# Zero products in one run, seven normalised tiles on ScalarE and seven centred tiles on VectorE, in a transformer block on one core

## The chip, the cores and the metric

One core of a Trainium2 chip. The metric is the device time in microseconds (us) of one execution; a profile's span, from the first to the last instruction, is somewhat shorter. The engines work side by side and meet at semaphores: TensorE (PE, matrix products; PEld is its loading of weights), VectorE (DVE), ScalarE (ACT), GpSimd (POOL), and SyncE (SP), which issues all transfers here.

## The reference

A pre-norm block: linear attention with a learned feature map (32 heads of 20), then a bilinear gated layer. Sequence 2048, width 640, inner width 1536, bf16.

```python
def _layernorm(x, axis=-1, eps=1e-5):
    m = jnp.mean(x, axis=axis, keepdims=True)
    v = jnp.var(x, axis=axis, keepdims=True)
    return (x - m) / jnp.sqrt(v + eps)

    # A: attention, with q, k, v = x @ wqkv, split in heads
    pk = jnp.einsum("bhsd,hdf->bhsf", k, w_phi)           # the same for q
    phi_k = jnp.concatenate([_softmax(pk), _softmax(-pk)], axis=-1)
    kv = jnp.einsum("bhsf,bhsd->bhfd", phi_k, v)
    z  = jnp.einsum("bhsf->bhf", phi_k)
    num = jnp.einsum("bhqf,bhfd->bhqd", phi_q, kv)
    den = jnp.einsum("bhqf,bhf->bhq", phi_q, z)[..., None] + 1e-6
    o = num / den                                         # heads joined, then @ wo

    # B: gated layer
    g = jnp.einsum("bsd,df->bsf", x, w_gate)
    u = jnp.einsum("bsd,df->bsf", x, w_up)
    return jnp.einsum("bsf,fd->bsd", g * u, w_down)

    h = x + _A_ref(_layernorm(x), A_wqkv, A_w_phi, A_wo)
    h2 = h + _B_ref(_layernorm(h), B_w_gate, B_w_up, B_w_down)
```

## The kernel before

The sequence is cut into 16 tiles of 128 rows. The program is a graph of named operations, each with an engine and the buffers that it reads and writes. A list scheduler in Python, which runs while the kernel is built, puts them into one fixed order for each engine, and derives the semaphore waits from it. What it goes by is a table with an entry for each operation: a key (a smaller key goes first among the operations that are ready) and, after a second colon, which of its allowed engines it takes (0, the default, is the one it is declared with, 1 the alternative). `xn3:13.372` is the normalisation of tile 3 with key 13.372 on its declared engine.

The names that matter here: `x` loads of rows, `wk`, `wv` loads of weights, `warm` products of zeros whose result nobody reads, `PH` and `PS` small products that lay the feature weights out, `WT` transposes of wk blocks on TensorE, `F1` folds of the feature weights into wk, `L1` statistics of the first layernorm, `xn` its normalised rows, `xt` their transpose (on TensorE for tiles 0 to 2, by a DMA from tile 3 on), `V`, `K`, `KV` the projections and the product of keys and values, `hc` the centred rows of the second layernorm, `hT` their transpose by DMA, `U` and `D` the gated layer.

TensorE's first operations, with cuts:

```python
NWARM = 8
def warm(e):
    for _ in range(1):
        ins = e.matmul(pb(wm_b)[:, 0:512], lhsT=T["zero"][:, 0:P], rhs=T["zero"][:, :], start=True, stop=True)
    return ins
for k in range(NWARM):
    G.op("pe", "warm%d" % k, warm, 0.43 if k < 7 else 0.22, LT, [z_b], [wm_b], -90)
# ...
G.op("pe", "PH", rows, 1.9, LT, [w32_b, id_b], [pq_b], -95)      # 40 products of 16 columns
# PHd: a copy of PH's result into phid
G.op("pe", "PS", spread, 0.6, LT, [es_b, pd_b], [pr_b], -95)     # 14 products
# PHe: a copy of PS's result into Phi; WT0..4, F1_0..4 follow
```

With the table of before, TensorE runs warm0 to warm3, PH, warm4 to warm6, PS, WT0, WT1, xt1, WT4, xt0, warm7, and then the folds F1 and the first V.

The first layernorm. VectorE makes mean and variance of each tile, ScalarE the reciprocal root as exp(-0.5 ln(v + eps)) for a group of up to four tiles, VectorE the normalised rows:

```python
G.op("dve", "L1s%d" % t, l1, ...)                   # two bn_stats over 320 columns each
G.op("dve", "L1a%d" % t, ...)                       # bn_aggr -> mv[t] = mean, variance
for tl in LNG:                                      # [0] [1] [2,3] [4..7] [8..11] [12..15]
    G.op("act", "L1l%d" % a, ...)                   # Ln
    G.op("act", "L1e%d" % a, ...)                   # Exp -> rs
def xn(e, t=t, xb=xb):
    return e.tensor_scalar(out=rev(xb), in0=T["x"][:, t, :].rearrange("p (c n) -> p c n", c=NC),
                           scalar1=T["mv"][:, t, 0:1], scalar2=T["rs"][:, t:t + 1], op0=ALU.subtract, op1=ALU.mult)
G.op("dve", "xn%d" % t, xn, 0.5, LD, [x_b[t], mv_b[t], rs_b[t]], [xb], 10 * t - 22)
```

The second layernorm. The rows are only centred here (mean minus row); the scale comes in at the end, when the gated layer's result is multiplied by 1/(v + eps), since the layer is of second degree in its input.

```python
G.op("act", "hc%d" % t, lambda e, t=t, hc=hc: e.activation(
    out=rev(hc), in_=T["x"][:, t, :].rearrange("p (c n) -> p c n", c=NC), func=AF.Identity, scale=-1.0, bias=T["mv2"][:, t, 0:1]),
    act_c(640, True), LA, [x_b[t], m2], [hc], kk)
```

`xn` and `hc` share four row buffers. All transfers, the transposes by DMA among them, are issued by SyncE in one fixed order, so an issue that waits for its data holds those behind it.

Of the kernel before, what the change touches and what calls it, by code (L numbers as in the profile page):

```python
# [6 lines left out]
FP32 = mybir.dt.float32  # L7
# [5 lines left out]
P = 128  # L13
# [29 lines left out]
NWARM = 8  # L43
# [5 lines left out]
x0:1.66 wk0:2.14 wk2:4.06 wk4:2.62 x1:1.18 wv0:3.58 wv2:4.54 wv4:5.98 x2:3.1 x4:5.02 x6:5.5 w32:0.7 x8:15.272 x10:22.162 x12:29.242 x14:21.682  # L49
wqt0:25.582 wqt1:26.802 wqt2:34.322 wqt3:35.542 wqt4:39.202 wqt5:40.422 wo0:55.782 wo2:58.182 wg0:55.302 wu0:56.742 wg1:54.822 wu1:57.222 wg2:53.382  # L50
wu2:57.702 wg3:54.342 wu3:58.662 wg4:53.862 wu4:56.262 id0:0.95 gl0:0.7 eps:1.25 id1:1.45 gla0:4.88 glb0:5.25 gla4:4.22 glb4:4.66 gla1:2.67 glb1:4.44
gla2:2.89 glb2:3.33 gla3:3.11 glb3:3.8 va1:1.85 glx:5.62 kv1:6.02 zero:0.7 warm0:1.08 warm1:1.51 warm2:1.94 warm3:2.37 warm4:4.7 warm5:5.13 warm6:5.56
warm7:8.153 es0:3.55 es1:4.02 PH:2.8 PHd:4.97 PS:5.99 PHe:6.86 WT0:6.59 WTe0:7.483 WT1:6.925 WTe1:8.213:1 WT2:10.4 WTe2:11.005:1 WT3:10.735
WTe3:11.657:1 WT4:7.539 WTe4:8.144:1 F1_0:8.423 Fe1_0:9.567:1 F1_1:9.227 Fe1_1:10.813 F1_2:12.157 Fe1_2:12.728:1 F1_3:13.002 Fe1_3:13.574 F1_4:8.809
Fe1_4:10.19:1 L1s0:4.686 L1a0:5.686 L1s1:3.823 L1a1:5.506 L1s2:9.867 L1a2:10.867 L1s3:9.047 L1a3:10.687 L1s4:11.732 L1a4:15.192 L1s5:12.552 L1a5:16.761
L1s6:15.302 L1a6:16.541 L1s7:14.372 L1a7:16.651 L1s8:26.422 L1a8:28.172 L1s9:20.982 L1a9:29.812 L1s10:25.602 L1a10:27.242 L1s11:27.352 L1a11:29.702
L1s12:38.952 L1a12:40.592 L1s13:39.772 L1a13:43.052 L1s14:40.702 L1a14:42.942 L1s15:30.382 L1a15:32.702 L1l0:6.016 L1e0:6.446 L1l1:5.796 L1e1:6.236
L1l2:11.437 L1e2:12.387 L1l4:17.051 L1e4:17.894 L1l8:30.102 L1e8:30.532 L1l12:43.63 L1e12:44.06 xn0:7.046 xt0:7.874 xte0:8.629:1 xn1:6.546 xt1:7.26
xte1:8.943 xn2:13.872 xt2:15.205 xte2:16.122:1 xn3:13.372 xt3:14.052 xn4:19.062 xt4:20.462 xn5:24.642 xt5:28.022 xn6:18.562 xt6:19.242 xn7:23.682
xt7:24.362 xn8:31.702 xt8:33.102 xn9:32.202 xt9:37.982 xn10:31.202 xt10:31.882 xn11:34.232 xt11:36.762 xn12:46.002 xt12:46.942 xn13:50.762 xt13:52.162  # L60
xn14:45.042 xt14:45.722 xn15:50.262 xt15:50.942 V0_0:9.777 V0_1:10.048 V0_2:11.342 V0_3:11.885 V0_4:13.847 Ve0:14.82 K0_0:15.484 K0_1:15.756
K0_2:16.028 K0_3:16.299 K0_4:16.571 Kx0_0:17.271 Kx0_1:18.104 Ks0:19.562 Kr0:21.802 Kn0:22.442 KV0:30.426 V1_0:11.07 V1_1:11.613 V1_2:12.458 V1_3:12.73
V1_4:13.304 Ve1:14.197 K1_0:13.575 K1_1:14.119 K1_2:14.39 K1_3:14.662 K1_4:14.934 Kx1_0:15.475 Kx1_1:16.309 Ks1:17.142 Kr1:25.142 Kn1:27.181 KV1:31.102
V2:16.843 Ve2:18.727 K2:18.201 Kx2_0:19.83 Kx2_1:20.663 Ks2:22.262 Kr2:24.182 Kn2:24.822 KV2:34.495 V3:19.56 Ve3:21.286 K3:20.918 Kx3_0:22.546
Kx3_1:23.38 Ks3:28.282 Kr3:29.922 Kn3:30.562 KV3:39.246 V4:26.351 Ve4:28.078 K4:24.993 Kx4_0:26.621 Kx4_1:27.455 Ks4:34.732 Kr4:37.572 Kn4:38.212
KV4:42.639 V5:33.137 Ve5:34.863 K5:31.778 Kx5_0:33.407 Kx5_1:34.24 Ks5:36.152 Kr5:38.032 Kn5:40.571 KV5:43.315 V6:23.635 Ve6:25.46 K6:22.276
Kx6_0:24.003 Kx6_1:24.836 Ks6:32.812 Kr6:38.492 Kn6:42.93 KV6:45.651 V7:29.068 Ve7:30.696 K7:27.71 Kx7_0:31.372 Kx7_1:32.206 Ks7:41.522 Kr7:43.162
Kn7:45.289 KV7:50.402 V8:36.529 Ve8:38.158 K8:39.922 Kx8_0:41.55 Kx8_1:42.384 Ks8:46.502 Kr8:49.342 Kn8:50.007 KV8:55.153 V9:41.28 Ve9:43.007 K9:44.292
Kx9_0:45.921 Kx9_1:46.754 Ks9:47.922 Kr9:49.802 Kn9:52.366 KV9:57.49 V10:35.171 Ve10:36.799 K10:37.888 Kx10_0:39.516 Kx10_1:40.349 Ks10:43.622
Kr10:45.542 Kn10:47.648 KV10:58.166 V11:46.327 Ve11:47.955 K11:47.685 Kx11_0:49.313 Kx11_1:50.147 Ks11:51.262 Kr11:54.102 Kn11:54.742 KV11:61.86  # L70
V12:51.078 Ve12:52.706 K12:52.437 Kx12_0:54.065 Kx12_1:54.898 Ks12:56.175 Kr12:58.511 Kn12:59.46 KV12:62.536 V13:58.842 Ve13:60.47 K13:55.829
Kx13_0:57.458 Kx13_1:58.291 Ks13:59.124 Kr13:60.724 Kn13:61.819 KV13:65.174 V14:53.795 Ve14:55.423:1 K14:49.043 Kx14_0:50.77 Kx14_1:51.603 Ks14:52.682
Kr14:54.562 Kn14:57.101 KV14:65.85 V15:63.514 Ve15:65.142 K15:60.2 Kx15_0:61.828 Kx15_1:62.662 Ks15:63.495 Kr15:65.095 Kn15:65.735 KV15:70.843
KVe0:73.009 KVe1:71.789 KVe2:72.399 F0_0:61.558 Fe0_0:62.13:1 F0_1:63.212 Fe0_1:63.784 F0_2:64.872 Fe0_2:65.555:1 F0_3:57.188 Fe0_3:57.76:1 F0_4:43.991
Fe0_4:44.562 Q0_0:69.764 Qx0_0_0:71.113 Qx0_0_1:71.629 Q0_1:71.519 Qx0_1_0:72.868 Qx0_1_1:73.385 Q0_2:67.605 Qx0_2_0:68.954 Qx0_2_1:69.471 Q0_3:66.526
Qx0_3_0:68.392 Qx0_3_1:67.875 Q0_4:68.684 Qx0_4_0:70.55 Qx0_4_1:70.034 Q1_0:86.818 Qx1_0_0:89.397 Qx1_0_1:88.167 Q1_1:76.87 Qx1_1_0:78.736
Qx1_1_1:78.22 Q1_2:89.945 Qx1_2_0:91.811 Qx1_2_1:91.295 Q1_3:73.677 Qx1_3_0:75.543 Qx1_3_1:75.026 Q1_4:72.598 Qx1_4_0:73.947 Qx1_4_1:74.464 Q2_0:77.95
Qx2_0_0:79.815 Qx2_0_1:79.299 Q2_1:91.025 Qx2_1_0:94.591 Qx2_1_1:93.041 Q2_2:92.104 Qx2_2_0:94.075 Qx2_2_1:93.558 Q2_3:81.532 Qx2_3_0:82.881
Qx2_3_1:83.398 Q2_4:94.886 Qx2_4_0:96.235 Qx2_4_1:96.752 Q3_0:79.374 Qx3_0_0:80.723 Qx3_0_1:81.24 Q3_1:80.453 Qx3_1_0:82.319 Qx3_1_1:81.802 Q3_2:83.301
Qx3_2_0:84.65 Qx3_2_1:85.167 Q3_3:75.791 Qx3_3_0:77.657 Qx3_3_1:77.14 Q3_4:85.739 Qx3_4_0:87.605 Qx3_4_1:87.088 wd0:97.348 wd1:100.008 wd2:99.528  # L80
wd3:97.828 N0_1:79.029 N0_0:75.101 sr0:79.644 rho0:80.134 A0:80.504 B0:81.534 dd0:82.564 rd0:82.954 o0:83.434 oT0:84.855 O0:87.897 h0:89.525
L2s0:90.587 L2a0:91.597 L2v0:91.887 L2r0:92.627 hc0:92.328 hT0:93.251 N1_1:74.756 N1_0:75.446 sr1:75.371 rho1:76.061 A1:76.431 B1:77.461 dd1:78.491
rd1:78.881 o1:79.361 oT1:80.782 O1:84.38 h1:86.311 L2s1:87.273 L2a1:88.393 L2v1:88.683 L2r1:89.305 hc1:88.684 hT1:90.705 N2_1:82.956 N2_0:82.611
sr2:83.571 rho2:84.061 A2:84.431 B2:85.461 dd2:87.063 rd2:88.093 o2:88.573:1 oT2:89.485 O2:93.183 h2:94.811 L2s2:95.873 L2a2:96.883 L2v2:97.173
L2r2:97.913 hc2:97.269 hT2:98.308 N3_1:89.255 N3_0:89.6 sr3:90.277 rho3:91.407 A3:91.777 B3:92.807 dd3:93.837 rd3:94.227 o3:94.707 oT3:96.128
O3:101.913 h3:103.541 L2s3:104.503 L2a3:106.475 L2v3:107.074 L2r3:107.505 hc3:106.765 hT3:108.444 N4_1:99.585 N4_0:100.476 sr4:100.336 rho4:101.091
A4:101.461 B4:102.663 dd4:104.293 rd4:105.323 o4:105.803 oT4:107.224 O4:112.293 h4:113.921 L2s4:115.025 L2a4:116.596 L2v4:116.886 L2r4:117.556
hc4:116.886 hT4:117.81 N5_1:104.708 N5_0:103.271 sr5:105.623 rho5:106.285 A5:106.655 B5:107.685 dd5:108.917 rd5:109.307 o5:109.787 oT5:111.208
O5:114.197 h5:115.845 L2s5:117.686 L2a5:118.716 L2v5:119.006 L2r5:120.68 hc5:119.006 hT5:119.93 N6_1:94.541 N6_0:95.965 sr6:95.563 rho6:96.693
A6:97.063 B6:98.093 dd6:99.123 rd6:99.685 o6:100.165 oT6:101.586 O6:122.42 h6:124.049 L2s6:124.98 L2a6:125.98 L2v6:126.27 L2r6:126.742 hc6:126.724  # L90
hT6:127.647 N7_1:135.54 N7_0:135.195 sr7:136.155 rho7:137.083 A7:137.891 B7:138.921 dd7:140.39 rd7:141.218 o7:141.698 oT7:143.119 O7:150.494 h7:152.309
L2s7:153.792 L2a7:155.23 L2v7:155.52 L2r7:156.029 hc7:155.52 hT7:156.444 N8_1:122.075 N8_0:125.937 sr8:123.097 rho8:126.552 A8:126.922 B8:128.662
dd8:130.332 rd8:130.722 o8:131.202 oT8:132.975 O8:139.122 h8:141.828 L2s8:142.77 L2a8:144.44 L2v8:144.73 L2r8:145.47 hc8:145.195 hT8:146.118
N9_1:140.825 N9_0:140.48 sr9:141.518 rho9:142.58 A9:143.59 B9:144.62 dd9:145.65 rd9:146.04 o9:146.52:1 oT9:147.431 O9:155.09 h9:156.827 L2s9:157.759
# [128 lines left out]
def build_graph():  # L223
# [20 lines left out]
    def rev(b):  # L244

        return T["xn"][:, b.slots[0], :].rearrange("p (c n) -> p c n", c=NC)[:, ::-1, :]
# [100 lines left out]
    for k in range(NWARM):  # L347
        G.op("pe", "warm%d" % k, warm, 0.43 if k < 7 else 0.22, LT, [z_b], [wm_b], -90)
# [696 lines left out]
```

## Time and profile before

| | |
|---|---|
| device time, median of three runs | 286.63 us |
| span of the profiled execution | 285.1 us |
| VectorE busy | 181.3 us (64%) |
| ScalarE busy | 107.4 us (38%) |
| GpSimd busy | 58.1 us (20%) |
| transfers | 22.33 MB, mean 78 GB/s |

A page of the profile gives each engine's busy time, the span in equal slices, the chain of work that ended last (from the last instruction back to what released it, step by step), groups of instructions by line and tile, and the waits: who waited for whom. A PE row's busy time is a modelled one[...]. L461 is line 461 of the kernel: L345 the zero products, L361 `PH`, L381 `PS`, L396 `WT`, L417 the folds, L469 `xt` on TensorE, L490 `V` and `K`, L528 `KV`, L433 and L434 the statistics, L461 `xn`, L644 `hc`, L519 the key normalisation on GpSimd, L614 that of the attention's output, L625 the product with wo, L664 and L683 the gated layer.

### The profile page before, as it was taken

What the parts mean: (1) busy time and instruction counts of PE and PEld (TensorE: products, weight loads), DVE (VectorE), ACT (ScalarE), POOL (GpSimd) and SP (SyncE); (2) the same over time, 40 slices, a digit from 0 to 9 for tenths busy, and PEclk for the clock granted to TensorE, in tenths of its full rate; (3) what the DMA queues carried; (4) which work ended last, traced back from release to release, by engine and by line L of the source; (5) the groups of instructions that cost most, each with busy time, mean ns of one, the idle gap of its engine ahead of it and who ended that gap; (6) DMA issues with size and microseconds to landing.
All of it is one profiled execution on the core that took longest, in us unless ns stands there. A gap on an engine that the chain in (4) does not pass through costs nothing.

```text
span 285.1 us, 5142 instructions
## 1 busy us (share of the span) xinstructions
PE 279.8 (98%) x2137; PEld 186.7 (65%) x2137; DVE 181.3 (64%) x368; ACT 107.4 (38%) x189; POOL 58.1 (20%) x65
## 2 busy tenths in 40 slices
PE   8999989999999999999999999999999999999996
PEld 4976758788555688875555574445776544587884
DVE  4598998986258789878497981157765223722242
ACT  3787646644787753122423123032020233211210
POOL 5005629897111322100120000000011000000000
PEclk9999999999999999999999999999999999999999
DMA  6728584599002675242212231000132010110002
GB/s 173 247 69 158 121 108 80 72 294 390 7 2 46 72 210 162 45 82 58 46 25 46 48 70 46 1 2 0 48 92 75 19 23 1 25 46 22 27 0 71
DMA packets 44216, 22.33 MB, mean 78 GB/s; under 512 B 35328, under 2 KB 42912, under 8 KB 44192
## 3 DMA queue, kind: packets, MB, share of 16 engines
q1 hardware_dynamic: 44192, 21.99, 32.5%
q8 instruction: 17, 0.28, 0.4%
q14 instruction: 7, 0.06, 0.1%
HBM read 11.00 MB, written 2.62 MB: 48 GB/s over the span
## 4 chain that ended last, share of the span: by engine, by line
PE 90%; DVE 4%; DMA 3%; ACT 1%; issue 0%; SPq 0%; DVEq 0%
PE ps L664 36%; PE ps L683 18%; PE ps L490 8%; PE ps L625 8%; PE ps L549 8%; PE ps L582 4%; PE ps L528 3%; DMA xnT<-xn 2%; DVE SR L514 2%; DMA x_all<-in_A_x_dram 1%; PE ps L345 1%; PE ps L417 1%; PE ps L396 1%; DVE xn L461 1%; DVE st L434 1%; DVE st L433 1%
## 5 line engine op out<-in xcount | busy, mean ns | idle before, releaser
L664 PE MATMUL ps<-xnT,Wgu 128*128 128x512 bf16 (+1 forms) x600 | 107.6, 336 | 0.0
L664 PEld LDWEIGHTS ps<-xnT,Wgu 128*128 128x128 bf16 x600 | 58.2, 98 | 42.9 <-DVE ev L672 0.2
L669 ACT ACTIVATE scratch<-ps 128x512 bf16<-128x512 f32 (+1 forms) x60 | 30.6, 511 | 102.0 <-PE ps L664 92.0
L672 DVE TENSOR_TENSOR ev<-ps,scratch 128x512 bf16<-128x512 f32 (+1 forms) x60 | 32.9, 575 | 40.5 <-PE ps L664 23.8
L683 PE MATMUL ps<-Wp,ev 128*128 128x320 bf16 (+2 forms) x396 | 54.0, 295 | 0.0
L490 PE MATMUL ps<-Wp,xnT 128*128 128x320 bf16 x320 | 46.1, 299 | 1.7 <-DMA xnT<-xn 1.7
L683 PEld LDWEIGHTS ps<-Wp,ev 128*128 128x128 bf16 x396 | 38.0, 98 | 14.1
L519 POOL TENSOR_TENSOR ev<-ev,SR 128x1280 bf16<-128x1280 bf16 x16 | 37.3, 2356 | 29.5 <-DVE SR L517 29.4
L490 PEld LDWEIGHTS ps<-Wp,xnT 128*128 128x128 bf16 x320 | 30.4, 98 | 13.3 <-DMA xnT<-xn 2.3
L614 POOL TENSOR_TENSOR scratch<-scratch,sm 128x640 bf16<-128x640 f32 x10 | 12.7, 1270 | 79.3 <-DVE sm L611 79.3
L695 DVE SCALAR_TENSOR_TENSOR Wp<-ps,rs,x_all 128x640 bf16<-128x640 f32 (+3 forms) x18 | 14.6, 810 | 21.6 <-PE ps L683 21.4
L558 ACT ACTIVATE eqT<-ps 128x512 bf16<-128x512 f32 x40 | 21.6, 596 | 8.8 <-PE ps L549 8.8
L511 ACT ACTIVATE ev<-ps 128x640 bf16<-128x640 f32 x32 | 20.9, 700 | 9.6 <-PE ps L490 9.6
L625 PE MATMUL ps<-Wo,scratch 128*128 128x320 bf16 x160 | 24.3, 299 | 0.0
L514 DVE TENSOR_REDUCE SR<-ev 128x64 f32<-128x1280 bf16 x16 | 23.3, 1466 | 0.9 <-ACT ev L511 0.8
L644 ACT ACTIVATE xn<-x_all,mv 128x640 bf16<-128x640 bf16 x16 | 13.2, 825 | 28.2 <-DVE mv L638 28.2
L549 PE MATMUL ps<-xnT,Wp 128*128 128x512 bf16 x100 | 22.9, 379 | 0.0
L625 PEld LDWEIGHTS ps<-Wo,scratch 128*128 128x128 bf16 x160 | 15.5, 98 | 7.3 <-DMA scratch<-scratch 0.3
L639 POOL TENSOR_SCALAR ln<-mv 128x1 f32<-128x1 f32 x16 | 3.9, 243 | 78.3 <-DVE mv L638 78.3
L629 DVE TENSOR_TENSOR x_all<-ps,x_all 128x640 bf16<-128x640 f32 x16 | 13.1, 821 | 9.8 <-PE ps L625 9.5
L549 PEld LDWEIGHTS ps<-xnT,Wp 128*128 128x128 bf16 x100 | 9.6, 98 | 10.0 <-DVE KVm L535 0.2
L582 PE MATMUL ps<-KVm,eqT 128*128 128x154 bf16 (+1 forms) x192 | 15.2, 221 | 0.0
(61 smaller groups left out, 208.2 us busy)
## 6 DMA issues: line engine op xcount, KB each, us to landing
out_dram<-Wp SPq DMA_DIRECT2D x15, 160.0 KB, 1.8
x_all<-in_A_x_dram SPq DMA_DIRECT2D x7, 320.0 KB, 3.7
Wgu<-in_B_w_gate_dram SPq DMA_DIRECT2D x5, 384.0 KB, 4.8
Wgu<-in_B_w_up_dram SPq DMA_DIRECT2D x5, 384.0 KB, 9.0
Wp<-in_B_w_down_dram SPq DMA_DIRECT2D x4, 480.0 KB, 4.7
scratch<-in_A_wqkv_dram SPq DMA_DIRECT2D x2, 320.0 KB, 5.3
Wp<-in_A_wqkv_dram SPq DMA_DIRECT2D x2, 320.0 KB, 5.8
Wo<-in_A_wo_dram SPq DMA_DIRECT2D x1, 480.0 KB, 10.2
```

The costliest lines, as they stand in the source:

```text
L490: ins = e.matmul(pb(b, hb)[:, 0:320], lhsT=T["xnT"][:, NC - 1 - c, P * t:P * (t + 1)], rhs=T["Wp"][:, kind, c, 320 * hb:320 * (hb + 1)], s ...
L511: G.op("act", "Kx%d_%d" % (t, s), lambda e, s=s, b=b, ek=ek: e.activation(out=T["ek"][:, ek.slots[0], s, :].rearrange("p (b n) -> p b n", ...
L514: G.op("dve", "Ks%d" % t, lambda e, ek=ek, sr=sr: e.tensor_reduce(out=T["SR"][:, sr.slots[0], 0, :], in_=T["ek"][:, ek.slots[0], :, :].rea ...
L519: G.op("pool", "Kn%d" % t, lambda e, ek=ek, sr=sr: e.tensor_tensor(out=T["ek"][:, ek.slots[0], :, :].rearrange("p s (h f) -> p (s h) f", f ...
L549: ins = e.matmul(pb(b)[:, 0:n], lhsT=T["Wp"][:, 0, i, P * c:P * (c + 1)], rhs=T["xnT"][:, NC - 1 - i, o0:o0 + n], start=(i == 0), stop=(i ...
L558: G.op("act", "Qx%d_%d_%d" % (q, c, s), lambda e, s=s, c=c, o0=o0, n=n, b=b: e.activation(out=T["eqT"][:, s, c, o0:o0 + n], in_=pb(b)[:, 0 ...
L582: ins = e.matmul(pb(b, y)[:, 22 * h0:22 * (h0 + j1 - j0)], lhsT=T["eqT"][:, s, c, P * t:P * (t + 1)], rhs=T["KVm"][:, OFF[s, c] + j0:OFF[s ...
L625: ins = e.matmul(pb(b, hb)[:, 0:320], lhsT=T["oT"][:, oT.slots[0], c, :], rhs=T["Wo"][:, c, 320 * hb:320 * (hb + 1)], start=(c == 0), stop ...
L664: ins = e.matmul(pb(b)[:, 0:n], lhsT=T["Wgu"][:, gu, c, P * ft:P * (ft + 1)], rhs=T["xnT"][:, NC - 1 - c, o0:o0 + n], start=(c == 0), stop ...
L669: G.op("act", "g%d_%d" % (bi, ft), lambda e, pg=pg, gt=gt, n=n: e.activation(out=T["gt"][:, gt.slots[0], 0:n], in_=pb(pg)[:, 0:n], func=AF ...
L672: o_ = G.op("dve", "u%d_%d" % (bi, ft), lambda e, pu=pu, gt=gt, hh=hh, ft=ft, n=n: e.tensor_tensor(out=T["hh"][:, hh.slots[0], ft, 0:n], i ...
L683: ins = e.matmul(pb(b, hb)[:, 0:w], lhsT=T["hh"][:, hh.slots[0], ft, P * tt:P * (tt + 1)], rhs=T["Wd"][:, ft, c0 + w * hb:c0 + w * (hb + 1 ...
```

## The change

It does three things, and comes with a new table.

1. *Zero products in one run.* Ten instead of eight. Eight run one after the other ahead of the small products `PH`; the other two stand between `PH` and `PS`. The aim is that TensorE is kept busy without a break from its first product on.
2. *Normalised rows on ScalarE.* `xn` may now run there too, as x * rstd + bias with bias = -mean * rstd. The bias is made by a one-column product on GpSimd for each tile from 3 on, and `xn` waits for it wherever it runs. The table picks ScalarE for tiles 3, 5, 7, 8, 9, 10 and 14. The aim is to take work from VectorE in the first stage.
3. *Centred rows on VectorE.* `hc` may now run there, as (x - mean) * -1. The table picks VectorE for tiles 5, 6, 7, 9, 10, 11 and 15.

```diff
-NWARM = 8
+NWARM = 10
     for k in range(NWARM):
-        G.op("pe", "warm%d" % k, warm, 0.43 if k < 7 else 0.22, LT, [z_b], [wm_b], -90)
+        G.op("pe", "warm%d" % k, warm, 0.43 if k < 8 else 0.22, LT, [z_b], [wm_b], -90)
-    G.op("pe", "PH", rows, 1.9, LT, [w32_b, id_b], [pq_b], -95)
+    G.op("pe", "PH", rows, 1.5, LT, [w32_b, id_b], [pq_b], -95, before=[G.by["warm7"]])
-    G.op("pe", "PS", spread, 0.6, LT, [es_b, pd_b], [pr_b], -95)
+    G.op("pe", "PS", spread, 0.8, LT, [es_b, pd_b], [pr_b], -95)
+    for k in range(8, NWARM):
+        G.by["warm%d" % k].before.append(G.by["PH"])
+        G.by["PS"].before.append(G.by["warm%d" % k])
 ...
+        for t in tl:
+            if t not in TPE:
+                G.op("pool", "L1n%d" % t, lambda e, t=t: e.tensor_scalar(
+                    out=T["nb"][:, t:t + 1], in0=T["mv"][:, t, 0:1], scalar1=T["rs"][:, t:t + 1], scalar2=-1.0, op0=ALU.mult,
+                    op1=ALU.mult), 0.2, LP, [rs_b[t], mv_b[t]], [nb_b[t]], 10 * t - 25)
 ...
-        def xn(e, t=t, xb=xb):
+        def xn(e, eng="dve", t=t, xb=xb):
+            if eng == "act":
+                return e.activation(out=rev(xb), in_=T["x"][:, t, :].rearrange("p (c n) -> p c n", c=NC), func=AF.Identity,
+                                    scale=T["rs"][:, t:t + 1], bias=T["nb"][:, t:t + 1])
 ...
-        G.op("dve", "xn%d" % t, xn, 0.5, LD, [x_b[t], mv_b[t], rs_b[t]], [xb], 10 * t - 22)
+        G.op("dve", "xn%d" % t, xn, 0.5, LD, [x_b[t], mv_b[t], rs_b[t], nb_b[t]], [xb], 10 * t - 22,
+             alts=[] if t in TPE else [("act", act_c(640, True), LA)])
 ...
+        def hcf(e, eng, t=t, hc=hc):
+            i_ = T["x"][:, t, :].rearrange("p (c n) -> p c n", c=NC)
+            if eng == "dve":
+                return e.tensor_scalar(out=rev(hc), in0=i_, scalar1=T["mv2"][:, t, 0:1], scalar2=-1.0, op0=ALU.subtract, op1=ALU.mult)
+            return e.activation(out=rev(hc), in_=i_, func=AF.Identity, scale=-1.0, bias=T["mv2"][:, t, 0:1])
 ...
```

The whole table is new (84 lines before, cut here), so the order on every engine differs. By its keys, TensorE begins with warm0 to warm7, PH, WT4, xt0, warm8, warm9, WT3, PS, xt1, WT2, WT0, WT1, F1_4, F1_3, V1. The loads of wk all stand ahead of those of wv; the last three loads of x (`x10`, `x12`, `x14`) stand in a row; the DMA transposes of tiles 8 to 11 stand together, ahead of the last four of the six for the query weights, two of which stood between them before. Of the copies out of PSUM five change to VectorE (those after PH, WT1, tile 1's transposes, V15 and F0_1) and four to ScalarE (WT4, V14, F0_0, F0_3), and of the normalisations of the attention's output (L614) GpSimd takes thirteen instead of ten, VectorE three instead of six.

## The prediction

> **What bounds the kernel now.** I read the busy shares first, then the waits of the two TensorE rows, then a table of busy time in stretches, then the chain that ended last over its first 16 us. The busy shares (engine, busy us, share of the span, instructions):
>
> ```profile
> PE 279.8 (98%) x2137; PEld 186.7 (65%) x2137; DVE 181.3 (64%) x368; ACT 107.4 (38%) x189; POOL 58.1 (20%) x65
> ```
>
> TensorE is the bound, but 98% of a modelled end is no proof, so I look at what it waited for (engine, line, releaser: us in all, times, longest):
>
> ```profile
> PEld ps L345 <- DVE zero L340: 1.2, 1, 1.2
> PEld ps L490 <- DMA xnT<-xn: 2.3, 2, 1.7
> PEld ps L625 <- DMA scratch<-scratch: 0.3, 1, 0.3
> ```
>
> Only the projections of the first stage (L490) ever lose much, 2.3 us in two waits for a transposed tile of the normalised x. The stretches say where (stretch, then busy us and instructions of PE, PEld, DVE, ACT, POOL, then clock, DMA share, GB/s):
>
> ```profile
> 0.00:12.20 12.20, 10.95 (x110) 8.12 (x111) 5.24 (x14) 5.83 (x11) 4.24 (x23) 1.00 0.77 244
> ...
> 16.00:44.00 28.00, 26.32 (x220) 19.27 (x219) 26.34 (x54) 18.63 (x32) 12.35 (x6) 1.00 0.69 121
> 44.00:71.00 27.00, 27.00 (x308) 22.05 (x305) 22.46 (x29) 15.58 (x25) 23.91 (x11) 1.00 0.75 213
> 71.00:101.00 30.00, 30.00 (x206) 16.95 (x204) 18.77 (x42) 22.01 (x41) 5.85 (x6) 1.00 0.23 33
> ```
>
> From 44 us on TensorE is solid: after the last stretch with a hole, nothing that another engine does faster can end the kernel earlier. From 16 to 44 us VectorE is busy 26.34 of 28.00, and TensorE misses 1.68: there VectorE limits. Before 12.2 us TensorE looks busy too, but the chain shows with what (start, us, line, instructions):
>
> ```profile
> 1.25 1.89 PE ps L345 x4
> 3.14 1.63 PE ps L361 x40
> 4.77 1.39 PE ps L345 x3
> 6.16 1.50 PE ps L381 x14
> 7.66 1.39 PE ps L396 x12
> 9.05 0.53 PE ps L469 x5
> 9.59 0.64 PE ps L396 x6
> 10.23 0.53 PE ps L469 x5
> 10.76 0.43 PE ps L345
> 11.19 1.22 PE ps L417 x21
> 12.40 0.55 PE ps L490 x4
> 12.95 0.67 PE ps L396 x12
> ```
>
> The same twelve transposes of L396 take 1.39 us at 7.66 and 0.67 us at 12.95: 116 against 56 ns each. So TensorE ran at half its rate until some point between 10.8 and 12.9 us. The warming products are cut in three: four before the small products of L361, three after them, one at 10.76. Neither the first four nor the next three bring the full rate.
>
> [...] the centred rows[...] are measured at 825:
>
> ```profile
> L644 ACT ACTIVATE xn<-x_all,mv 128x640 bf16<-128x640 bf16 x16 | 13.2, 825 | 28.2 <-DVE mv L638 28.2
> L461 DVE TENSOR_SCALAR xn<-x_all,mv,rs 128x640 bf16<-128x640 bf16 x16 | 8.8, 581 | 1.5 <-ACT rs L444 1.5
> ```
>
> [...]
>
> **The change, part by part.**
>
> *Zero products in one run.* From the diff: eight of them first, then the small products (L361), then by the keys in the table one weight block's transposes (6), those of tile 0 (5), two more zero products, another block's transposes (6), the spreading products (L381), tile 1's transposes (5), three blocks' (18), two folds, and the first V product. Eight at 0.43 us (one alone at 10.76) from 1.25 end at 4.69. They cover 3.44 us without a hole, where before the longest run of them was 1.89. The small products, 1.63 us, end at 6.3. I choose that the full rate is there from then on. Then 17 transposes at 56 ns are 0.95, two zero products at half of 0.43 are 0.43, and the spread is an estimated 0.8 (half of 1.50): 8.5 us. 23 more transposes, 1.3: 9.8. Two folds at about 0.4 (21 products in 1.22 are three folds): 10.6 us for the first V product, against 12.40 now, so 1.8 us. What is then still open differs: now two blocks' transposes (0.67) and two folds (0.8); after, three folds (1.2), 0.27 us less. Gain at the front **2.1 us** if the rate is there by 6.3 us.
> If it comes only by about 8.5 us, 17 transposes cost 60 ns more each (1.0), the zero products 0.43 and the spread 0.7: 2.1 us, and the gain is nil. I give the early case 0.7, this one 0.25, still later 0.05, so the expected gain is about 0.7 x 2.1 = 1.5 us.
> The data just permit it: the transfers land in the order of their issue, in the kernel before wv's first two blocks at 9.1 and the last of wk after them at 10.0 us. The new order puts all of wk ahead of wv, so wk should be complete at about 9.1, when its first two blocks are wanted (tile 1's transposes and one block's come before them), and wv's first two at 10.0, ahead of the V product at 10.6. The copy out of the small products goes to VectorE.
>
> *Row normalisation on ScalarE, tiles 3, 5, 7, 8, 9, 10, 14.* VectorE loses seven instructions. Two in a row take 1.10 us and three 1.62, so about 0.54 each. Six fall in the stretch 16 to 44 or just before it: 26.34 - 6 x 0.54 = 23.1 of 28. [...] GpSimd gets thirteen products of one column for the bias (mean x rstd x -1), for every tile from 3 on, about 0.25 us each (its one-column addition takes 243 ns): 3.2 us, most of it between 16 and 44, where it is busy 12.35. They stand between Exp and the normalisation, also for tiles that stay on VectorE, which now wait for them as well; a bias may have to wait for a running 2.36 us product of L519.
> What this is worth is bounded by TensorE's waits, about 2 us. The second wait has this history in VectorE's timeline:
>
> ```profile
> 28.82 0.49 DVE L433 BATCH_NORM_STATS2 st<-x_all 128x6 f32<-128x320 bf16 x1 [1.36 <-DMA x_all<-in_A_x_dram]
> ...
> 34.07 1.62 DVE L461 TENSOR_SCALAR xn<-x_all,mv,rs 128x640 bf16<-128x640 bf16 x3
> ```
>
> Statistics wait for the load of x that was issued at 25.08 behind transposes; the normalisations end at 35.7, the transposed tile lands at 40.90, and TensorE starts again at 40.94. In the new table the last three loads of x stand in a row, and the four transposes of tiles 8 to 11 stand ahead of most of the query weights' transposes, so the path gets shorter at both ends. Against it, TensorE comes 1.5 to 2 us earlier and asks earlier. I count **1.4 us** of the 2.0 as saved, and 0.6 as left.
>
> *Centred rows on VectorE, tiles 5, 6, 7, 9, 10, 11, 15.* They are off the path: TensorE is full from 44 us on, and ScalarE has room. VectorE gets 7 x 0.54 = 3.8 us, and gives three of its normalising products (820 ns) to GpSimd, net +1.3 us over 150 us in which it is busy 19 to 26 us out of 30. Each saves one hop between engines. 0 us.
>
> *Sum.* 1.5 + 1.4 = 2.9, rounded up to 3.0 for the idle time that two less crowded engines may give back: 286.63 - 3.0 = **283.6 us**.
>
> **The rivals.**
> 1. *TensorE's clock comes no earlier.* [...] Then there is no front gain, and only the waits shrink: 285 to 287 us.
> 2. *The waits for transposed tiles stay or grow*, because the transfers' queue and not VectorE paces them: one issue of a transpose takes 1.2 to 1.3 us in the queue and some took 2.0 to 2.4. For: the tile that TensorE waited for took 4.9 us from issue to landing, others 2.6. Then the front gain is given back at about 30 to 40 us: 285.5 to 287.
> 3. *The one-column products on GpSimd hold normalisations back* behind 2.36 us products: a new wait of 1 to 2 us in the first stage, 285 to 288 us.
> 4. *Everything fits:* 2.1 + 2.0, and 0.3 from the wait of L625: 282.2 us.
>
> **Range and chances.** A gain above 5.7 us, which over 2% would need, is more than front and waits hold together (about 4.4), so faster gets 0.04. Slower by 2% would need 5.7 us of new waits in a stage that has no more than 2.3 now: 0.03. The range runs from rival 4 with a little over to rival 1 without gain: 281.8 to 286.6.
>
> **What would show it.** Right: the first projection at 10.3 to 11 us; twelve transposes near 0.67 us before 9.8 us; waits of L490 for transposed tiles under 1 us; VectorE at 22 to 24 us between 16 and 44; [...] PE solid after 44 us as now. Wrong: transposes still at 116 ns after 8 us (first step); a wait of L490 of over 2 us, or one for ScalarE or GpSimd (second step); holes in TensorE after 100 us at the first product of a block, released by a transposed centred row (third step).

## The result, and the profile after

The changed kernel takes 284.19 us (median of four; 283.92 to 284.61) against 286.63 us (286.45 to 287.33) for the kernel before on the same chip: ratio 0.991, 95% interval 0.9885 to 0.9936. Two executions in this document, one of the kernel before at 1035.1 us and one of `a_run13_old` at 326.35 us, stand far off all others, and the ratios leave them out. The forecast was 283.6 us, in a range of 281.8 to 286.6. Timed once more (run `a_again` below) the changed kernel has ratio 0.9941, interval 0.9928 to 0.9955. So the gain is 0.6 to 0.9%, or 1.7 to 2.6 us. The span of the profiled execution fell from 285.1 to 282.2 us.

The busy shares, as before (engine, busy us, share of the span, instructions):

```profile
PE 277.0 (98%) x2122; PEld 184.7 (65%) x2139; DVE 179.9 (64%) x366; ACT 106.7 (38%) x188; POOL 64.4 (23%) x81
```

They say almost nothing: TensorE was 98% and is 98%. What it waited for says more (PEld's waits in the changed kernel: engine, line, releaser: us in all, times, longest; L506 is now the projections, L641 the product with wo, L485 a tile's transposes on TensorE):

```profile
PEld ps L506 <- DMA xnT<-xn: 0.9, 2, 0.7
PEld ps L641 <- DMA scratch<-scratch: 0.7, 1, 0.7
...
PEld ps L485 <- DVE xn L476: 0.5, 1, 0.5
```

The waits for transposed tiles fell from 2.3 to 0.9 us. The stretches, with the columns of before (PE, PEld, DVE, ACT, POOL busy, then clock, DMA share, GB/s):

```profile
0.00:12.20 12.20, 10.90 (x141) 8.02 (x143) 8.16 (x21) 7.27 (x14) 4.17 (x23) 1.00 0.76 242
...
16.00:44.00 28.00, 27.64 (x239) 20.56 (x238) 26.98 (x53) 23.42 (x40) 18.95 (x19) 1.00 0.69 130
44.00:71.00 27.00, 26.95 (x285) 20.89 (x285) 17.05 (x18) 16.26 (x27) 21.19 (x10) 1.00 0.76 208
71.00:101.00 30.00, 29.66 (x215) 18.06 (x216) 21.43 (x48) 21.99 (x42) 4.45 (x6) 1.00 0.26 44
```

In the first 12.2 us TensorE has 141 products instead of 110 in the same busy time; from 16 to 44 us it misses 0.36 instead of 1.68 us. VectorE is not emptier there (26.98 against 26.34), but has 17.05 us of work in the next stretch where it had 22.46. TensorE's timeline shows the front (start, us, line, tile, shape, count):

```profile
1.24 3.24 PE L349 MATMUL ps<-zero 128*128 128x512 bf16 x8 [1.24 <-DVE zero L344]
4.41 1.69 PE L365 MATMUL ps<-ident,w 32*20 32x16 bf16 x40
...
8.66 1.17 PE L403 MATMUL ps<-ident,scratch 128*128 128x128 bf16 x18
9.67 0.75 PE L424 MATMUL ps<-Phi,scratch 120*128 120x120 bf16 x14
10.27 0.70 PE L506 MATMUL ps<-Wp,xnT 128*128 128x320 bf16 x4
```

The eighteen transposes start at 8.66 us and the next group at 9.67, so they take 56 ns each; before, they took 116 ns each until 9 us, and the full rate of 56 ns shows only at 12.95. The first V product starts at 10.27 instead of 12.25 us. The trace's clock record begins to grant the full rate at 3.99 us; in the kernel before that was at 11.79.

In this one pair of traces the last product starts 2.9 us earlier (279.56 against 282.47): 2.0 from the front, up to the first V product, and 0.9 from all that follows, which the shorter waits would explain. The experiments ask whether that attribution holds.

### The profile page after: what moved, and what is told of

It is laid out like the page before. It is cut to its first block, busy times and chain, and to the rows that moved or that the text cites. A ratio compares the mean times of both kernels' runs of the same rounds, so it can differ in the third digit from the quotient of the medians.

```text
span 282.2 us, 5153 instructions
## 1 busy us (share of the span) xinstructions
PE 277.0 (98%) x2122; PEld 184.7 (65%) x2139; DVE 179.9 (64%) x366; ACT 106.7 (38%) x188; POOL 64.4 (23%) x81
## 4 chain that ended last, share of the span: by engine, by line
PE 88%; DMA 6%; SPq 2%; ACT 1%; DVE 1%; issue 1%; POOL 0%; DVEq 0%
PE ps L683 37%; PE ps L702 18%; PE ps L506 12%; PE ps L641 7%; PE ps L565 6%; PE ps L598 4%; PE ps L544 3%; DMA x_all<-in_A_x_dram 3%; SPq L275 2%; DMA scratch<-scratch 2%; DMA xnT<-xn 2%; ACT xn L474 1%; ACT ev L239 1%; PE ps L424 1%; POOL scratch L630 0%
## 5 line engine op out<-in xcount | busy, mean ns | idle before, releaser
L683 PE MATMUL ps<-xnT,Wgu 128*128 128x512 bf16 (+1 forms) x588 | 105.7, 336 | 0.6
L506 PE MATMUL ps<-Wp,xnT 128*128 128x320 bf16 x320 | 46.1, 299 | 0.4 <-DMA xnT<-xn 0.4
L506 PEld LDWEIGHTS ps<-Wp,xnT 128*128 128x128 bf16 x320 | 30.3, 98 | 12.0 <-DMA xnT<-xn 0.9
L630 POOL TENSOR_TENSOR scratch<-scratch,sm 128x640 bf16<-128x640 f32 x13 | 16.5, 1270 | 67.5 <-DVE sm L627 62.0
L641 PE MATMUL ps<-Wo,scratch 128*128 128x320 bf16 x160 | 24.0, 299 | 0.2 <-DMA scratch<-scratch 0.2
L655 POOL TENSOR_SCALAR ln<-mv 128x1 f32<-128x1 f32 x16 | 3.3, 209 | 83.7 <-DVE mv L654 74.6
L641 PEld LDWEIGHTS ps<-Wo,scratch 128*128 128x128 bf16 x160 | 15.5, 98 | 7.6 <-DMA scratch<-scratch 0.7
L598 PEld LDWEIGHTS ps<-KVm,eqT 128*128 128x128 bf16 x192 | 12.8, 98 | 3.5
```

The lines of the kernel that those rows point to most:

```text
L506: ins = e.matmul(pb(b, hb)[:, 0:320], lhsT=T["xnT"][:, NC - 1 - c, P * t:P * (t + 1)], rhs=T["Wp"][:, kind, c, 320 * hb:320 * (hb + 1)], s ...
L598: ins = e.matmul(pb(b, y)[:, 22 * h0:22 * (h0 + j1 - j0)], lhsT=T["eqT"][:, s, c, P * t:P * (t + 1)], rhs=T["KVm"][:, OFF[s, c] + j0:OFF[s ...
L641: ins = e.matmul(pb(b, hb)[:, 0:320], lhsT=T["oT"][:, oT.slots[0], c, :], rhs=T["Wo"][:, c, 320 * hb:320 * (hb + 1)], start=(c == 0), stop ...
L683: ins = e.matmul(pb(b)[:, 0:n], lhsT=T["Wgu"][:, gu, c, P * ft:P * (ft + 1)], rhs=T["xnT"][:, NC - 1 - c, o0:o0 + n], start=(c == 0), stop ...
```

## The experiments

**How they were built.** The scheduler's order is fixed first, and then single operations are placed elsewhere in it or left out, so nothing else changes place on any engine. Each ratio is to the kernel before, timed beside the variant on the same chip. The edits are lines that run after `order, _ = schedule(G)`; `place(order, op, engine, start)` puts an operation at the given place.

**1. The run of zero products alone, in the old order (`b_run`).**

```diff
+for k in range(4, 8):
+    place(order, by["warm%d" % k], "pe", by["PH"].start - 0.01 + 0.001 * k)
```

> The kernel before, with its eight zero products in one run ahead of the small products; nothing else moves on any engine. Theory (two separate gains, about 2 us at the front from TensorE's clock and about 1 us from shorter waits for transposed tiles): the full rate comes at about 4 us instead of 11.8, the first V product starts at 10.3 to 10.8 us instead of 12.25, the two waits of L490 stay at about 2 us together, and the time is 285.0 us, 2.0 less. Rival (VectorE and the transfers pace the first stage): the front comes earlier too, but the waits of L490 grow by as much, to 3.5 to 4 us, and the time is 286.3 to 287.

Measured: 287.26 us, ratio 1.0025 (1.0012 to 1.0038). Neither theory: slower, and not by waits of L490 (0.9 us on PEld's row of its trace). In the profiled execution the full rate came only at 12.95 us and the first V product at 13.20. The run does not by itself bring the rate in every execution.

**2. The run cut up again, in the new order (`a_split`).**

```diff
+leave_out(G, order, ["warm8", "warm9"])     # warm7 takes warm8's place
+for k in range(4, 7):
+    place(order, by["warm%d" % k], "pe", by["PH"].start + 0.001 * k)
```

> The changed kernel, with its zero products cut as in the kernel before: four, the small products, three, and one more where the ninth stood; the tenth and ninth left out; nothing else moves. Theory: full rate only at about 11 to 12 us, first V product at 12.0 to 12.8 instead of 10.27, the wait for a transposed tile at 39 us vanishes because TensorE comes later, time 285.7 to 286.4, 1.5 to 2.2 more than with the run. Rival (the new order and engines made the front, not the run): first V product before 11 us, time 284.0 to 284.6.

Measured: 285.66 us, ratio 0.9972 (0.995 to 0.9994), but the times spread from 283.6 to 288.1. The median lies at the lower edge of the theory's range, but the spread is twice that of before (285.3 to 287.4, 75 executions), and some executions without the run are as fast as the fastest with it. In the profiled execution, the slowest, the rate came at 13.87 us and the first V product at 13.60, later than the theory said. So with the run cut up again 0.3% of the gain is left, which the rest of the change must bring.

**3 and 4. The engine moves undone, each alone (`a_xn_dve`, `a_hc_act`).** The seven normalised rows return to VectorE, without the one-column products; in the other kernel the seven centred rows return to ScalarE.

```diff
+leave_out(G, order, [n for n in G.by if n.startswith("L1n")])
+for t in (3, 5, 7, 8, 9, 10, 14):
+    place(order, by["xn%d" % t], "dve", by["xn%d" % t].start)
```
```diff
+for t in (5, 6, 7, 9, 10, 11, 15):
+    place(order, by["hc%d" % t], "act", by["hc%d" % t].start)
```

> The changed kernel, with the normalisation of all tiles back on VectorE, each of the seven placed in VectorE's order where the schedule had it on ScalarE, and without the thirteen one-column products on GpSimd; order otherwise unchanged. Theory (the engine of these rows shortens the waits): VectorE gets 7 x 0.54 = 3.8 us more before 45 us, the waits of the projections for transposed tiles go from about 0.9 to about 2 us, time 285.0 to 285.6. Rival (the new order of loads and transposes does it, the engine is indifferent): waits within 0.3 us of 0.9, time 284.0 to 284.5.

> The changed kernel, with all sixteen centred rows back on ScalarE, in its order where the schedule had them on VectorE; nothing else moves. Theory (they are off the path): time within 0.2 us of the changed kernel's 284.2, no hole in TensorE after 100 us. Rival (the engine change matters, as it saves a hop before a transpose): a wait of the gated layer for a transposed row of 0.3 to 1 us, time 284.6 to 285.2.

Measured: 285.35 us, ratio 0.9964 (0.9944 to 0.9983), and 284.91 us, ratio 0.9954 (0.9933 to 0.9975). Again a spread of 4 us: 283.56 to 287.61 and 283.55 to 287.54, with the same lowest time. In both profiled executions, which were late ones, the first V product starts at 14.06 and 14.03 us. The waits for transposed tiles are 0.6 us in the trace of `a_xn_dve` and 0.5 in that of `a_hc_act`, so they did not grow to 2 us with all rows on VectorE. The spread of the times hides the rest of what was asked, so its cause comes first.

**5. What spreads the times.** The clock records begin to grant the full rate at 3.99 us in the trace of the changed kernel, 11.79 in that of the kernel before, 12.95 in that of `b_run` and 13.87 in that of `a_split`. The kernels of 3 and 4 have the changed kernel's front, eight zero products in one run ahead of the small ones, and yet the first V product of their traces starts 3.8 us later than its 10.27. So one and the same front may have the rate early in one execution and late in another. How often was an estimate of mine, the 55% in the first expectation below. `a_again` and `a_run13` put that to the test, the latter with thirteen zero products ahead of the small ones.

```diff
+by["warm0"].emit = four products instead of one     # a_run13: 13 ahead of PH, none after
+place(order, by["warm8"], ...); place(order, by["warm9"], ...)
```

> The changed kernel itself, timed again. [...] Theory[...]: eight zero products release the rate by 5.6 us in some 55% of executions and otherwise only at 13 to 14 us, so the times fall into two heaps, 283.5 to 284.7 and 285.2 to 287.6, with a median of 284.5 to 285.3. Rival (the first four times, 283.9 to 284.6, are the kernel's): all but a few times under 284.8.

> The changed kernel with thirteen zero products ahead of the small products and none after them; nothing else moves. Thirteen at half rate are 5.5 us[...]. Theory[...]: the rate is there by 7.5 us in every execution, no time over 285.5, all within about 1.2 us, median 284.0 to 284.8, the later start of the small products costing up to 0.5 us. Rival (the spread has another cause): as wide as the changed kernel's, 4 us, and the median up by the five products' time, 1 to 2 us.

Measured for `a_again`: 284.70 us; six times of 284.47 to 284.88, and two of 286.30 and 288.68. Two heaps, but six to two; over both timings ten of twelve are early. (The kernels of 3 and 4 with the same front had 21 of their 44 times below 285.1, without a clear gap between two heaps.) The profiled execution was the latest one, and its front is that of half rate:

```profile
1.24 3.60 PE L349 MATMUL ps<-zero 128*128 128x512 bf16 x8 [1.24 <-DVE zero L344]
...
11.18 2.13 PE L403 MATMUL ps<-ident,scratch 128*128 128x128 bf16 x18
13.10 1.06 PE L424 MATMUL ps<-Phi,scratch 120*128 120x120 bf16 x14
14.01 0.70 PE L506 MATMUL ps<-Wp,xnT 128*128 128x320 bf16 x4
```

The same eighteen transposes take 1.92 us up to the next group, 107 ns each, and the first V product is 3.7 us later than in the early execution. Late, the changed kernel starts its V products after the kernel before (12.25): the small products wait behind eight zero products, until 4.77 us instead of 3.14.

Measured for `a_run13`: 285.41 us, ratio 0.9977 (0.9954 to 1.0001), 284.28 to 287.59. Wrong: five of fourteen are late. Those five, and no others, show a mean granted clock of 0.994. Over 285 us that is some 3.4 us at half rate (an estimate: 0.006 x 285 / 0.5). The rate comes and is lost again.

**6. The rate can be lost (`b_run13`, `a_run13_old`).**

```diff
+for k in range(4, 8): ...                            # b_run13: warm4 to warm7 placed ahead of PH, as in 1
+by["warm0"].emit = six products instead of one      # 13 ahead of PH in the old order
```

> The kernel before with thirteen zero products in one run ahead of the small products, in place of four, three and one; nothing else moves, so the order, the loads and the engines are those of before. The rate is there early in every execution. Theory A (a fast front is worth 2 us in any order): 284.3 to 285.0. Theory B (the old order is paced by VectorE and the transfers from 16 to 44 us, so that an early front is given back as waits of L490): 285.4 to 286.3, waits of L490 of 2.5 to 4 us.

> The changed kernel with thirteen zero products ahead, and with both engine moves undone: all normalised rows on VectorE, without the one-column products, and all centred rows on ScalarE. What stays is the new table's order and the zero products. Theory (the order makes the gain, the engines of these rows are indifferent): within 0.3 us of the same kernel with the moves. Rival (the normalisation on ScalarE shortens the waits): 0.7 to 1.5 us more.

`b_run13`: 288.15 us, ratio 1.0052 (1.0025 to 1.0079), against both theories. Stretches of its trace show why (columns as above; the number ahead of the DMA share is the granted clock):

```profile
1.38:4.79 3.41, 3.41 (x9) 1.21 (x8) 1.19 (x3) 0.70 (x1) 3.19 (x16) 1.00 0.68 170
4.79:8.21 3.42, 2.79 (x46) 1.88 (x43) 0.73 (x4) 0.59 (x1) 0.47 (x1) 1.00 0.89 276
8.21:11.62 3.41, 3.17 (x31) 3.17 (x32) 1.12 (x2) 2.25 (x8) 0.00 (x0) 0.50 1.02 366
11.62:15.03 3.41, 3.41 (x38) 3.18 (x37) 2.43 (x6) 2.64 (x5) 0.00 (x0) 0.50 0.18 65
15.03:18.45 3.42, 3.42 (x43) 2.83 (x42) 3.02 (x10) 2.41 (x6) 0.00 (x0) 1.00 0.00 0
```

The first row is zero products at half rate, before the record of the granted clock begins (its 1.00 is only the lack of a record). The second has the full rate, but holds the small products and a wait of 0.9 us for their copy: PE busy 2.79 of 3.42. At 8.21 the rate is gone, until 15.03; these 6.82 us at half rate are the 0.012 that the mean clock of this execution, 0.988, lacks. Two of its nine executions kept the rate (mean clock 1.00; 285.89 and 286.02 us), three have 0.994 and four 0.988. `b_run` shows the same: eight of 22 executions with 0.993 or 0.994. These are its eight fastest (285.51 to 286.87 us, against 286.88 to 288.09 for the others; the profiled one, with the rate only at 12.95 us, took 287.19), so there a rate that comes and is lost again seems still better than one that comes late. The old order, with nothing to run between the small products and the spread, mostly did not hold what thirteen zero products brought: seven of nine executions lost it. In the changed kernel, transposes and two zero products stand there, and its early trace kept the rate for 279.9 us without a break.

`a_run13_old`: 286.15 us, ratio 0.9991 (0.9965 to 1.0017), against 285.41 with the moves. Among executions with a mean clock of 1.00, taken as those that kept the rate, the medians are 285.56 (nine) and 285.16 (nine). That is between the theory and its rival, and the times of both still spread.

**7. Ten ahead and two between (`a_run10`), and the engine moves again on that footing.** Ten products should bring the rate early more often than eight, and two between them and the spread should hold it.

```diff
+by["warm0"].emit = three products instead of one    # 10 ahead of PH; warm8, warm9 stay after it
```

> The changed kernel with ten zero products ahead of the small products instead of eight, and its two between them and the spreading products kept; nothing else moves. [...] Theory[...]: [...] the two products between hold it; at most two times in ten over 285.8, the early heap 0.2 to 0.6 above the changed kernel's, median 284.4 to 285.2. Rival (the length of the run doesn't matter): as many late times as the changed kernel, four or five in ten over 285.8.

> The same with ten ahead, and all centred rows of the second layernorm back on ScalarE. Theory (off the path): median within 0.3 us of the same kernel with seven of them on VectorE. Rival (VectorE's share saves a hop): 0.4 us or more slower.

> The same with ten ahead, and all normalised rows of the first layernorm back on VectorE, without the one-column products on GpSimd. Theory (the new order of loads and transposes shortens the waits, the engine hardly): median within 0.3 us of the same kernel with seven on ScalarE. Rival (the engine shortens the waits): 0.7 to 1.5 us slower.

`a_run10`: 284.68 us, ratio 0.9942 (0.992 to 0.9963), 284.32 to 285.63: no time over 285.8, as expected. `a_run10_hc`: 284.67 us, ratio 0.9937 (0.9912 to 0.9962). The centred rows' engine makes no difference.

`a_run10_xn`: 285.45 us, ratio 0.9951 (0.9932 to 0.9971), in two heaps again: six times up to 284.77 and seven from 285.45 to 286.48. The lower heap equals `a_run10`; the upper is missing there, and in `a_run10_hc`: twelve of their thirteen times are at most 285.21. The intervals overlap. The stretch 16 to 44 us, first of `a_run10`, then of `a_run10_xn`:

```profile
16.00:44.00 28.00, 27.23 (x234) 20.11 (x233) 26.72 (x52) 23.22 (x41) 18.09 (x19) 1.00 0.72 126
```
```profile
16.00:44.00 28.00, 27.14 (x233) 19.97 (x232) 27.97 (x55) 19.48 (x35) 16.12 (x7) 1.00 0.75 129
```

VectorE without a gap (27.97 of 28.00) costs TensorE next to nothing (27.14 against 27.23). So the traces show no gain from the move. The times leave one open: the three comparisons point the same way, by 0.8 us here, by 0.4 in 6, and in 3 and 4 by 0.7 between the medians of the times below 285.1 (284.5 in `a_xn_dve`, 283.8 in `a_hc_act`). Each alone is small against the spread, and no trace shows where such a gain would come from.

**8. The early rate, held, in the old order (`b_fill`).**

```diff
+by["warm0"].emit = seven products   # with warm1..3: 10 ahead of PH
+by["warm4"].emit = five products    # with warm5, 6: 7 between PH and PS
```

> The kernel before with ten zero products ahead of the small products, seven between them and the spreading products, where TensorE waited 1.0 us in the earlier attempts and lost the rate again, and one at its old place; order, loads and engines are those of before. Theory A (the early, kept rate is the gain, in any order): most times 284.3 to 285.2. Theory B (the old order gives an early front back as waits of L490 between 16 and 45 us, or never starts its V products before their weights): most times 285.5 to 286.4, although the trace shows the rate granted by 8 us and kept.

Measured: 286.06 us, ratio 0.9995 (0.9972 to 1.0018), from 284.93 to 288.00. The profiled execution took 285.07 us, with the rate from 3.94 us on and ten more zero products than before. Its stretch and its wait for transposed tiles:

```profile
16.00:44.00 28.00, 28.00 (x238) 20.83 (x237) 27.23 (x55) 19.95 (x34) 13.54 (x6) 1.00 0.65 127
```
```profile
PEld ps L490 <- DMA xnT<-xn: 0.3, 1, 0.3
```

In the old order, with all rows normalised on VectorE (busy 27.23), TensorE misses nothing from 16 to 44 us. The waits of the kernel before are gone, with none of the engine moves. They were short already in `b_run`, whose first V product came later than before the change:

```profile
16.00:44.00 28.00, 27.93 (x242) 20.92 (x241) 26.25 (x54) 20.13 (x34) 11.31 (x5) 1.00 0.64 119
```

Theory B's reason is wrong in the trace of `b_fill`; of theory A's times (284.3 to 285.2) only two of fourteen came. Whether the other twelve had the rate late can't be read from their mean clock, which leaves out what lies ahead of the record: the late profiled execution of `a_again` has 1.00 as well.

## Why the prediction was right, and where it was not

**The number** came out (2.4 us between the medians against the 3.0 predicted, 1.8 in the second timing), by a sum of which one term stands in the early executions, one has no cause that was shown, and one omission was not small. Part of it is luck. That the first four times were all early has a chance of about one in eleven, if 31 in 56 are early (below); by the mean of its eight times the second timing gains 1.0 us (285.37 against 286.37).

**The front.** The working assumed the full rate from 6.3 us and got the first V product at 10.6 us; it came at 10.27, with the rate at 3.99. The step is right and the size too, 2.0 us at the first V product. What failed is the weighing. The prediction gave a rate by 8.5 us a chance of 0.25 and no gain, and one still later 0.05 and no cost; in the trace of the late execution the rate comes at 13.78 us and the first V product at 14.01, 1.8 us later than before the change. It is early in ten of twelve executions of the changed kernel, and in 31 of 56 (times below 285.1) together with the two kernels of the same front; what decides it was not shown. The median hides this; the mean would not.

**"Zero products in one run" as the cause** was half of it. By `b_run` the run of eight alone is 0.25% slower, by `a_split` the change without the run is 0.3% faster, and the two together gain 0.6 to 0.9%, more than their sum. One thing that the new order adds is work behind the small products: transposes and two zero products between them and the spread. With thirteen zero products ahead and none between, five of fourteen executions have a mean clock of 0.994; with ten and two (`a_run10` and its two variants), all 26 have 0.999 or 1.00. The prediction took those two products for a cost of 0.43 us and saw no use in them. It is not all: `b_fill` puts seven zero products there in the old order, and its ratio is 0.9995; with ten more zero products ahead, its first V product starts at 11.87 us even in an early execution. What else in the new order brings the gain was not taken apart.

**The normalised rows.** Predicted: waits from about 2 to 0.6 us; measured 2.3 to 0.9. Predicted: VectorE at 22 to 24 us between 16 and 44; measured 26.98. This step failed: VectorE filled the freed time with later tiles' work, which then was missing from 44 to 71 us (17.05 against 22.46). That the shorter waits came from the engine was not borne out: in `b_fill` they are 0.3 us without it, in `a_run10_xn` TensorE loses 0.1 us from 16 to 44 by undoing it. Over all traces but that of before they are 0.3 to 1.5 us with every row on VectorE and 0.5 to 1.6 with seven rows on ScalarE (1.6 in `a_again`, the changed kernel itself). Nor do they follow the front: they are 0.9 us in `b_run`, whose first V product came 1 us later than before. The time from the first V product to the last product says the same: 270.2 us in the kernel before, 269.3 and 270.3 in two traces of the changed kernel, 268.8 in `b_fill`. So the 0.9 us of the first pair of traces is no more than two executions of one kernel differ by, and the 1.4 us that the prediction counted here is not shown; why tile 8 came late in the trace of before stays open.

The costs: 918 ns for a row on ScalarE, 264 ns for each one-column product, put at 0.25 us, and a wait of 0.2 us in all for them (the groups of the changed kernel: line, engine, tile, count | busy us, mean ns | idle time before, releaser):

```profile
L474 ACT ACTIVATE xn<-x_all,nb,rs 128x640 bf16<-128x640 bf16 x7 | 6.2, 918 | 0.0
L476 DVE TENSOR_SCALAR xn<-x_all,mv,rs 128x640 bf16<-128x640 bf16 x9 | 5.0, 564 | 0.2 <-POOL nb L455 0.2
L455 POOL TENSOR_SCALAR nb<-mv,rs 128x1 f32<-128x1 f32 x13 | 3.2, 264 | 13.4 <-ACT rs L451 13.4
```

**The centred rows** were put at 0 us: 284.67 against 284.68.

**The rivals.** The first (the clock comes no earlier) happens, in a share of the executions of one and the same kernel. The second (waits that stay or grow) is not in the early trace; in the late one, `a_again`, they are 1.6 us against 2.3 before. The third (one-column products that hold rows back) is in neither: a single wait of 0.2 and 0.3 us. The fourth (everything fits, 282.2 us) did not come: the lowest time of the changed kernel is 283.92. None of these variants beats the changed kernel by more than the spread.

## What to carry to other kernels

A run of products that only warms TensorE can bring the full rate in one execution and not in the next: eight brought it at 3.99 us in one trace of the changed kernel, and in another (`a_again`) it came at 13.78. Nor is a rate that has come there to stay: in `b_run13` it was lost from 8.21 to 15.03 us, after small products and a wait of 0.9 us. So look at the work right after such a run as well as at its length: with ten zero products ahead and two between, none of 26 executions (`a_run10`, `a_run10_hc`, `a_run10_xn`) has a mean clock below 0.999; with thirteen ahead and none between (`a_run13`), five of fourteen have 0.994. Time a kernel often enough to see whether its times lie in one heap or two, and look at the clock of the profiled execution before believing a pair of traces. An engine that is nearly full in a stretch need not be what bounds it (in `a_run10_xn` VectorE is busy 27.97 of 28.00 us, and TensorE 27.14, against 27.23 in `a_run10`): the test is whether TensorE loses anything when that engine gets more to do.

## What the runs showed of the hardware

TensorE ran at two rates: a transpose took 116 ns at 7.66 us and 56 ns at 12.95 in the kernel before, a zero product 0.43 us there (at 10.76) and 0.22 in `b_fill` (at 10.66). The forty small products took 1.63 us at half rate (before, 3.14 to 4.77) and 1.62 at the full one (`b_fill`, 4.89 to 6.51).

The clock records begin to grant the full rate at 3.99 us (changed kernel), 3.94 (`b_fill`), 11.79 (before), 12.95 (`b_run`), 13.78 (`a_again`) and 13.87 (`a_split`). The first and the fifth are two executions of one kernel, with the same eight zero products from 1.24 us on. The rate was lost from 8.21 to 15.03 us in `b_run13`, after a stretch with PE busy 2.79 of 3.42 us, so that busy time did not foretell it. What decides when the rate comes and whether it stays was not shown.
